# Retention with first ranks as tasks of a list scheduler, a state of 128 full partitions, and five warming products

## The chip, the cores and the metric

The kernel runs on one core of a Trainium2 chip. Its time is device time in microseconds (us), from a launch to its end. Five engines have their own instruction streams, each run strictly in order: TensorE (PE; its weight loads PEld), VectorE (DVE), ScalarE (ACT), GpSimd (POOL) and SyncE (SP). An engine that waits for a value holds up everything behind it in its stream. DMAs are issued from SyncE's queue above all.

## What is computed

Three layers, one behind the other. Retention over 2 batches, 8 heads, 768 positions, 64 columns per head; then a mixture of 8 experts over 1536 tokens of 512 columns, in which each expert gets exactly 192 tokens; then a dense layer with ELU.

```python
for b in range(nb):                       # retention, per batch and head
    intra = einsum('bhic,bhjc->bhij', qb, kb) * Dmask   # lam ** (i - j), i >= j
    intra = einsum('bhij,bhjd->bhid', intra, vb)
    inter = einsum('bhid,bhde->bhie', qb * lam_pow, kv_state)
    out[:, :, sl] = intra + inter
    kv_state = lam_block * kv_state + einsum('bhsd,bhse->bhde', kb * rev_pow, vb)

logits = x @ w_gate                       # experts
for idx in argsort(-logits.flatten()):    # greedy: best pairs first, 192 per expert
    ...
for e in range(E):
    out[mask] = maximum(x[mask] @ w1[e], 0) @ w2[e]

h = x @ w_in                              # dense
out = where(h > 0, h, exp(minimum(h, 0)) - 1) @ w_out
```

## The kernel before

**Tiling.** Retention goes over 12 chunks of 128 positions (6 per batch; n is the chunk, c its number within the batch). Per chunk k and q are transposed on TensorE and copied out by ScalarE (kT, qT); `scores` makes 8 products of 64 rows into two banks; VectorE masks them with the decay (`masks`); `inter` multiplies the running state with the scaled q (qS); `intra` adds the masked scores times v; `state` multiplies the decayed k (kD) with v, and VectorE adds the result to the decayed old state (`new_state`, sD). The state is kept as 128x128 blocks per pair of heads, of which only the two 64x64 corners are filled; so it is written in two steps of 64 partitions, and `inter` is 4 full products. ScalarE copies the output (xT), TensorE turns it back (`natural`, xN), and it goes to DRAM (xd).

**First ranks.** A token's rank is the count of tokens whose best logit beats its own. So per chunk `scored` makes 8 logits per token, `logits` copies them and finds the best logit m and its expert (four small VectorE steps: m, t, wv, oh), `new_row` spreads m over all partitions (mrow), `compare_new` and `compare_old` compare the new chunk with all earlier ones, and `count` sums the comparisons on TensorE.

**Dense pieces.** w_in and w_out are 64 bit; 16 pieces of 1 MB are loaded (`load_dense`) and split into a high and a low half (`split_steps`: three VectorE steps, one copy on ScalarE, one VectorE step). Three pieces are split beside the retention, two more are loaded there, and the rest is done among the experts.

**Order.** In the retention the order of VectorE and TensorE is written out by hand: each function gets an offset from its chunk's number, and the steps are sorted by it (`steps`). ScalarE, GpSimd and SyncE follow from the program's general order. Behind that, `Plan` sets the order: a list scheduler with a cost per task, that takes at each step the task with the longest tail among those that can start soonest. Its ranks of expert 0 (`choose`) end in the index products (L835), ahead of which 12 warming products of ones stand in TensorE's stream (L872), and 16 behind.

**Tables.** The powers of lambda are made by doubling on VectorE (rt, L194), sent to DRAM (rtd) and read back as the scale of q (qsc); the decay matrix (dec, L202) comes from 8 scans. The loads of the second chunk stand behind these on SyncE's queue.

## Time and profile before

| | |
|---|---|
| median of 3 runs (lowest, highest) | 545.36 us (544.83, 548.29) |
| the profiled execution, and its span | 544.31 us, 542.5 us |
| busy in the span: TensorE, its weight loads | 512.8 us (95%), 434.9 us (80%) |
| busy in the span: VectorE, ScalarE, GpSimd | 372.0 us (69%), 290.0 us (53%), 103.2 us (19%) |
| chain that ended last, by engine | TensorE 64%, VectorE 14%, DMA 7%, issue 5%, ScalarE 4%, GpSimd 3% |

The busy share is a mean over stages with different limits, so each stage is read by itself. The chain of work is followed back from the last instruction to what released it. A row of windows names the busy time of TensorE, its weight loads, VectorE, ScalarE and GpSimd in this order, then the granted clock as a share of 2.4 GHz. "Idle before" is time for which an engine stood still ahead of an instruction, with what ended it.

### The profile page before, as it was taken

The page shows a single profiled execution, that of the slowest core. Times are in us where ns is not written, and L with a number is a line of the kernel's source. Part 1 is how long each engine was busy: PE and PEld are TensorE (multiplying, and loading weights), DVE is VectorE, ACT ScalarE, POOL GpSimd, SP SyncE. Part 2 cuts the span into 40 slices and gives each one's busy share as a digit, 9 for nine tenths or more (in the row PEclk, how much of TensorE's full clock was granted, in tenths as well). Part 3 has the DMA queues.
Part 4 walks back from the last instruction along what each step waited for, and adds up shares of the span by engine and source line. Part 5 has one row for each costly group of instructions (what it writes and reads, how often), then busy time and mean ns, then how long its engine had stood idle before and what let it go on. Part 6 is the DMA issues. An engine that isn't in the chain of part 4 may idle for free.

```text
span 542.5 us, 12848 instructions
## 1 busy us (share of the span) xinstructions
PE 512.8 (95%) x5308; PEld 434.9 (80%) x5308; DVE 372.0 (69%) x847; ACT 290.0 (53%) x556; POOL 103.2 (19%) x143
## 2 busy tenths in 40 slices
PE   6989899889899989999999999999999999999994
PEld 5878888879899975569959964997898489879941
DVE  7499899797989979698477665747647653572410
ACT  2335442332894584363984595459539533961910
POOL 5232420200116500230343010012401001000000
PEclk9899989799899999999999999999999999999999
DMA  6998961287486610460541045051405505050000
GB/s 133 242 226 205 263 214 46 69 279 323 132 292 218 225 33 2 185 212 3 187 141 44 17 171 174 22 185 22 158 4 187 174 21 185 3 174 2 2 19 21
DMA packets 62763, 70.70 MB, mean 130 GB/s; under 512 B 40184, under 2 KB 45264, under 8 KB 61680
## 3 DMA queue, kind: packets, MB, share of 16 engines
q1 hardware_dynamic: 59744, 63.21, 36.8%
q0 software_dynamic: 2960, 6.66, 3.6%
q8 instruction: 42, 0.69, 0.5%
q14 instruction: 17, 0.14, 0.1%
HBM read 63.34 MB, written 6.52 MB: 129 GB/s over the span
## 4 chain that ended last, share of the span: by engine, by line
PE 64%; DVE 14%; DMA 7%; issue 5%; ACT 4%; POOL 3%; SPq 0%; POOLq 0%; ACTq 0%
PE ps_s L981 5%; PE ps_s L980 5%; PE ps_t L981 5%; PE ps_s L982 4%; PE ps_t L980 4%; PE ps_t L982 4%; PE ps_s L1150 3%; PE ps_s L1148 3%; PE ps_s L1149 3%; PE ps_t L1148 2%; PE ps_t L1149 2%; PE ps_t L1150 2%; PE ps_S L980 2%; PE ps_S L981 2%; PE ps_S L982 2%
## 5 line engine op out<-in xcount | busy, mean ns | idle before, releaser
L981 PE MATMUL ps_t<-yt,wih 128*128 128x192 f16 x208 | 51.4, 247 | 1.6 <-DVE yt L1067 1.6
L982 PEld LDWEIGHTS <-wil 128*128 128x128 f16 x512 | 50.4, 99 | 1.8 <-issue 1.7
L982 PE MATMUL ps_t<-yt,wil 128*128 128x192 f16 x208 | 51.5, 248 | 0.0
L980 PE MATMUL ps_t<-yt,wih 128*128 128x192 f16 x208 | 51.4, 247 | 0.0
L980 PEld LDWEIGHTS <-wih 128*128 128x128 f16 x512 | 50.7, 99 | 0.1
L981 PEld LDWEIGHTS <-wih 128*128 128x128 f16 x512 | 50.4, 99 | 0.2
L982 PE MATMUL ps_s<-yt,wil 128*128 128x192 f16 x200 | 49.7, 248 | 0.0
L981 PE MATMUL ps_s<-yt,wih 128*128 128x192 f16 x200 | 49.7, 248 | 0.0
L980 PE MATMUL ps_s<-yt,wih 128*128 128x192 f16 x200 | 49.7, 248 | 0.0
L668 POOL DMA_INDIRECT open<-rec,dest x27 | 34.4, 1274 | 57.8 <-DVE dest L657 26.4
L1150 PEld LDWEIGHTS <-gg 128*128 128x128 f16 x192 | 18.8, 98 | 23.5 <-DVE gg L1129 0.9
L1150 PE MATMUL ps_s<-woh,gg 128*128 128x512 f16 x96 | 36.4, 379 | 0.4 <-DVE gg L1129 0.4
L1149 PE MATMUL ps_s<-wol,gg 128*128 128x512 f16 x96 | 36.4, 379 | 0.0
L1148 PE MATMUL ps_s<-woh,gg 128*128 128x512 f16 x96 | 36.4, 379 | 0.0
L1129 DVE TENSOR_TENSOR gg<-el,gg 128x384 f16<-128x384 f32 x64 | 34.4, 553 | 1.7 <-ACT gg L1128 1.6
L1121 ACT ACTIVATE el<-el 128x384 f32<-128x384 f32 x64 | 33.5, 524 | 1.8
L1122 ACT ACTIVATE el<-el 128x384 f32<-128x384 f32 x64 | 33.5, 523 | 1.7
L972 DVE SCALAR_TENSOR_TENSOR w2p<-stg,w2p 128x1024 f16<-128x1024 f32 x24 | 28.4, 1224 | 8.6 <-ACT w2p L969 8.5
L1128 ACT ACTIVATE gg<-el 128x384 f16<-128x384 f32 x64 | 31.6, 511 | 5.1 <-DVE el L1123 4.8
L1149 PEld LDWEIGHTS <-gg 128*128 128x128 f16 x192 | 18.7, 98 | 19.0
L1148 PEld LDWEIGHTS <-gg 128*128 128x128 f16 x192 | 18.8, 98 | 18.9
L860 POOL DMA_INDIRECT xa<-xd,idx x8 | 8.6, 1078 | 129.1 <-DVE idx L841 128.5
(254 smaller groups left out, 1561.5 us busy)
## 6 DMA issues: line engine op xcount, KB each, us to landing
stg<-in_moe_w_dram SPq DMA_DIRECT2D x24, 1024.0 KB, 5.4
stg<-in_moe_w_out_dram SPq DMA_DIRECT2D x8, 1024.0 KB, 4.9
stg<-in_moe_w_in_dram SPq DMA_DIRECT2D x5, 1024.0 KB, 6.3
w1p<-in_moe_w_dram SPq DMA_DIRECT2D x8, 512.0 KB, 5.8
w2p<-in_moe_w_dram SPq DMA_DIRECT2D x8, 512.0 KB, 8.8
kn<-in_k_dram SPq DMA_DIRECT2D x12, 256.0 KB, 4.9
qn<-in_q_dram SPq DMA_DIRECT2D x12, 256.0 KB, 5.0
vn<-in_v_dram SPq DMA_DIRECT2D x12, 256.0 KB, 4.6
```

Source lines behind the costliest of these rows:

```text
L668: st = nc.gpsimd.indirect_dma_start(out=buf, out_offset=bass.IndirectOffsetOnAxis(ap=dest[:, c:c + 1], axis=0), in_=rec[:, c, :], in_offse ...
L972: nc.vector.scalar_tensor_tensor(part(1), T["t"][:, 1024 * z:1024 * z + 1024], sc, part(0), op0=OP.mult, op1=OP.subtract)
L980: nc.tensor.matmul(o, wh, xh, start=first, stop=False, skip_group_check=True)
L981: nc.tensor.matmul(o, wh, xl, start=False, stop=False, skip_group_check=True)
L982: nc.tensor.matmul(o, wl, xh, start=False, stop=last, skip_group_check=True)
L1121: a = add("ACT", 0.49, lambda: nc.scalar.activation(e_, e_, AF.Exp, scale=-1.0), a, ahead=EAHEAD)
L1122: a = add("ACT", 0.49, lambda: nc.scalar.activation(e_, e_, AF.Copy, scale=SG, bias=-SG), a, ahead=EAHEAD)
L1128: a = add("ACT", 0.49, lambda: nc.scalar.activation(gh, two(e_), AF.Copy), a, *free, ahead=EAHEAD)
L1129: a = add("DVE", 0.53, lambda: nc.vector.tensor_tensor(gl, two(e_), gh, op=OP.subtract), a, ahead=EAHEAD)
L1148: nc.tensor.matmul(p, GH[:, f, c], woh[:, f, :], start=f == 0, stop=False, skip_group_check=True)
L1149: nc.tensor.matmul(p, GH[:, f, c], wol[:, f, :], start=False, stop=False, skip_group_check=True)
L1150: nc.tensor.matmul(p, GL[:, f, c], woh[:, f, :], start=False, stop=f == RF2 - 1, skip_group_check=True)
```

## The change

**What it does.** Retention and first ranks become tasks of a second `Plan` (hp), for all five engines. `Plan.add` gets a mode: a task of another mode than the last one on its engine costs 0.12 more in the plan, and one of the same mode is preferred by 0.5. (1) The power table goes; the scale of q comes from 4 scans over lambda, loaded as lam2 by ScalarE's queue, as lambda and w_gate are too. (2) The state is kept as 128 partitions of 4 x 64 columns, so `new_state` and the decayed state are one step each, and `inter` is 8 products of 64 rows by 64 columns, into two banks; heads of odd pairs come out swapped, and `natural` turns them back with a permuted identity (swap). xT is copied in two halves. (3) The scaling of k goes from GpSimd to ScalarE, 8 activations of 128x64 a chunk; the scaling of q goes from VectorE to GpSimd. (4) Per chunk VectorE finds m alone; wv and oh come for groups of 4, 4, 3 and 1 chunks (`best`). (5) Five dense pieces are split beside the retention, two more loaded. (6) Ahead of the retention 10 warming products stand in place of 16; ahead of the index products of expert 0, 5 in place of 12. (7) Of the two copies of a whole expert's tokens (xt) the second goes to VectorE. (8) The zero fill on GpSimd takes 2 x 64 columns of a chunk's slots in place of all 320.

```diff
-EARLY = ((0, 1.35), (2.45, 3.8), (6.1, 7.25))
-NEXT = (8.3, 9.3)
-WARM = (12, 4, 12, 16)
+EARLY_N, NEXT = 5, 2
+LD, PITCH, BEHIND = (1.3, 1.1), 5.5, 2.0
+WARM = (10, 5, 16)
...
+    TURN, KEEP = 0.12, 0.5
...
-            t = max(near, key=lambda t: tail[t["n"]] + t["ahead"])
+            t = max(near, key=lambda t: tail[t["n"]] + t["ahead"] + (self.KEEP if mode.get(t["eng"]) == t["mode"] else 0.0))
...
+    lamb = consts.tile([128, H], FT)
+    nc.scalar.dma_start(lamb, bass.AP(tensor=lam.tensor, offset=lam.offset, ap=[[0, 128], [1, H]]))
+    lam2 = consts.tile([128, HP], FT)
+    for i in range(2):
+        nc.scalar.dma_start(lam2[64 * i:64 * i + 64], bass.AP(tensor=lam.tensor, offset=lam.offset + i, ap=[[0, 64], [2, HP]]))
...
-    while w < 128:
-        nc.vector.tensor_scalar(rt[:, O + w + 1:O + 2 * w + 1], rt[:, O + 1:O + w + 1], rt[:, O + w:O + w + 1], None,
-                                op0=OP.mult)
-        w *= 2
...
+    def q_scales():
+        for a in range(HP):
+            nc.vector.tensor_tensor_scan(qsc[:, a, :], lam2[:, a:a + 1].to_broadcast([128, 128]), nothing, 1.0,
+                                         op0=OP.mult, op1=OP.add)
...
+        for h in range(4 * z, 4 * z + 4):
+            nc.scalar.activation(KD[n][:, h, :], KN[n][:, h, :], AF.Copy, scale=dec[:, 4 * (h % 2) + h // 2, 127:128])
...
+        QS[n] = att.tile([128, HP, 128], FT, name="qS")
+        nc.gpsimd.tensor_tensor(QS[n], QT[n], qsc, op=OP.mult)
...
+        OP_[n] = p = bank("o"), bank("m")
+        for a in range(HP):
+            for s in range(2):
+                r, z = slice(64 * s, 64 * s + 64), s ^ (a & 1)
+                nc.tensor.matmul(p[a % 2][64 * z:64 * z + 64, 128 * (a // 2):128 * (a // 2) + 128], Sb[n % NC % 2][r, a, :],
+                                 QS[n][r, a, :], start=a < 2, stop=False, skip_group_check=True)
...
+        if n % NC:
+            nc.vector.tensor_add(sn, pv, SD[n])
...
+    def best(c0, c1):
+        sh = [128, c1 - c0, E]
+        l, t = R.L[:, c0:c1, :], t4[:, 0:c1 - c0, :]
+        nc.vector.tensor_tensor(t, l, m[:, c0:c1, None].to_broadcast(sh), op=OP.is_equal)
         nc.vector.tensor_tensor(t, t, e8b.to_broadcast(sh), op=OP.mult)
+        nc.vector.tensor_reduce(wv[:, c0:c1], t, axis=AX, op=OP.max)
+        nc.vector.tensor_tensor(oh[:, c0:c1, :], wv[:, c0:c1, None].to_broadcast(sh), e8b.to_broadcast(sh), op=OP.is_equal)
...
+            put((e, n), "PE", 0.46, lambda n=n, z=z: transposed(n, z), *of(("ld", nm, n), (e + "o", n - 1)), mode="A")
+            put((e + "o", n), "ACT", 0.58, lambda n=n, z=z: transposed_out(n, z), *of((e, n), ("scores", n - 2), ("qS", n - 2)))
...
+        ld = add("SP", 2.9, lambda i=i: load_dense(i), T["ld", "v", 1], use[i % 2])
...
-            for _ in range(WARM[2]):
-                w = add("PE", 0.22, lambda: warm(), w)
+            for _ in range(WARM[1]):
+                w = add("PE", 0.43, lambda: warm(), w)
...
+                    (nc.vector.tensor_copy if g else nc.scalar.copy)(
+                        xt.rearrange("p a r n -> p (a r n)").bitcast(FT).rearrange("p (r n) -> p r n", r=RD)[:, sl, :], pv)
```

**ScalarE, the start of its stream, before** (kT and qT are the copies of transposed k and q, xT that of a chunk's output, L its logits, xN the natural order):

```order
L292 ACT_TABLE_LOAD
L292 ACTIVATE kT<-ps_t_186 128x512
L305 ACTIVATE qT<-ps_t_196 128x512
L292 ACTIVATE kT<-ps_t_222 128x512
L305 ACTIVATE qT<-ps_t_232 128x512
L351 ACTIVATE xT<-ps_o 128x512
L428 ACTIVATE L<-ps_m 128x8
L292 ACTIVATE kT<-ps_t_292 128x512
L305 ACTIVATE qT<-ps_t_302 128x512
L383 ACTIVATE xN<-ps_x 128x512
```

and now (kD is the scaled k, lam_74 the tile lam2; an x is a repeat):

```order
L156 DMA lamb<-in_lam_dram 128x8
L159 DMA lam_74<-in_lam_dram 64x4x1 x2
L198 DMA wg<-in_moe_w_gate_dram 128x2x8
L198 DMA wg<-in_moe_w_gate_dram 64x2x8 x2
L294 ACT_TABLE_LOAD
L294 ACTIVATE kD<-kn,dec 128x64 x4
L288 ACTIVATE kT<-ps_t_164 128x512
L294 ACTIVATE kD<-kn,dec 128x64 x4
L288 ACTIVATE qT<-ps_t_178 128x512
L294 ACTIVATE kD<-kn,dec 128x64 x4
L288 ACTIVATE kT<-ps_t_191 128x512
```

The six loads of lambda and w_gate come first, and the first chunk's k is scaled, four heads at a time, ahead of the copies of kT and qT; the second chunk's likewise.

**VectorE, from the masks of the fifth chunk to its new state, before** (wol is where masked scores lie, f a dense piece's scratch, stg its load, w1p the comparisons, S the state):

```order
L326 TENSOR_TENSOR wol<-ps_s_541,dec 128x512
L326 TENSOR_TENSOR wol<-ps_s_542,dec 128x512
L252 TENSOR_SCALAR f_136<-stg_134 128x1024
L431 TENSOR_REDUCE m<-L 128x1
L433 SCALAR_TENSOR_TENSOR t_567<-L,m,e_90 128x8
L434 TENSOR_REDUCE wv<-t_567 128x1
L435 TENSOR_SCALAR oh<-e_90,wv 128x8
L312 TENSOR_TENSOR qS<-qT,qsc 128x512
L255 SCALAR_TENSOR_TENSOR f_136<-stg_134,f_136 128x1024
L452 TENSOR_SCALAR w1p<-mrow,m 128x384
L448 SCALAR_TENSOR_TENSOR w1p<-mrow,m,before 128x128
L485 TENSOR_TENSOR w1p<-mrow,m 128x3x128
```

and now:

```order
L311 TENSOR_TENSOR wol<-ps_s_543,dec 128x512
L311 TENSOR_TENSOR wol<-ps_s_544,dec 128x512
L404 TENSOR_REDUCE m<-L 128x1
L411 TENSOR_TENSOR t_140<-L,m 128x32
L412 TENSOR_TENSOR t_140<-t_140,e_85 128x32
L413 TENSOR_REDUCE wv<-t_140 128x4
L414 TENSOR_TENSOR oh<-wv,e_85 128x32
L425 TENSOR_SCALAR w1p<-mrow,m 128x384
L453 TENSOR_TENSOR w1p<-mrow,m 128x3x128
L421 SCALAR_TENSOR_TENSOR w1p<-mrow,m,before 128x128
L243 TENSOR_SCALAR f_119<-stg_117 128x1024
L356 TENSOR_TENSOR S_126<-ps_S,sD 128x256
```

The scaling of q is gone, t, wv and oh are replaced by four steps for four chunks (here the group's end), the dense step stands elsewhere, and the state is one step of 128 partitions.

**TensorE, between the counts and the index products of expert 0, before** (ohs are the slots, mt the chosen tokens):

```order
L460 LDWEIGHTS woh
L460 MATMUL ps_S<-oh,woh 128x8
L777 MATMUL ps_o<-th,onesf 128x16
L872 MATMUL ps_t_1429<-onesf 128x128 x12
L835 LDWEIGHTS ohs
L835 MATMUL ps_o<-mt,ohs 128x1
```

and now:

```order
L433 LDWEIGHTS woh
L433 MATMUL ps_t_1171<-oh,woh 128x8
L819 MATMUL ps_o<-th,onesf 128x16
L914 MATMUL ps_t_1475<-onesf 128x128 x5
L877 LDWEIGHTS ohs
L877 MATMUL ps_o<-mt,ohs 128x1
```

Only the number of products of ones has changed there.

## Rows read from the trace of the kernel before

**Rows 1.** Windows: busy us by engine (instructions), clock, DMA share, GB/s.
```profile
27.71:95.73 68.02, 62.79 (x843) 57.56 (x843) 63.80 (x142) 27.78 (x61) 19.28 (x26) 0.95 0.70 188
20.00:68.00 48.00, 43.26 (x535) 39.80 (x533) 40.77 (x92) 21.91 (x48) 17.01 (x24) 1.00 0.95 237
```

**Rows 2.** Chain that ended last: start, us, what.
```profile
2.38 3.35 DVE rt L194
...
9.77 4.24 DMA qn<-in_q_dram
...
27.71 1.29 DVE wol L326 x2
...
86.89 1.29 DVE wol L326 x2
...
95.73 0.27 DVE tp L762
...
98.33 5.10 PE ps_t L872 x24
103.43 0.59 PE ps_o L835 x24
...
111.36 0.88 ACT xt L910 x2
```

**Rows 3.** Timeline: start, us, engine, line, operation, count, idle before.
```profile
7.36 2.61 DVE L202 TENSOR_TENSOR_SCAN dec<-lamb,identf 128x128 f32<-128x128 f32 x8
...
14.15 0.94 PE L303 MATMUL ps_t<-identf,qn 128*128 128x128 f32 x4 [2.05 <-DMA qn<-in_q_dram]
...
18.86 0.39 PE L389 MATMUL ps_m<-wg,xT 128*128 128x8 f32 x2
...
39.04 1.06 PE L389 MATMUL ps_m<-wg,xT 128*128 128x8 f32 x8
...
41.30 1.06 PE L335 MATMUL ps_o<-qS,S 128*128 128x128 f32 x8
...
43.88 1.16 PE L321 MATMUL ps_s<-qT,kT 64*128 64x128 f32 x16
44.97 1.06 PE L389 MATMUL ps_m<-wg,xT 128*128 128x8 f32 x8
...
100.45 0.17 DVE L822 TENSOR_TENSOR mt<-me,tid 128x12 f16<-128x12 f32 x1
```

**Rows 4.** VectorE lines: count, busy, mean ns, idle before; 0 to 95.7 us.
```profile
L312 DVE TENSOR_TENSOR qS<-qT,qsc 128x512 f32<-128x512 f32 x10 | 6.9, 687 | 4.7 <-ACT qT L305 4.7
L374 DVE TENSOR_TENSOR S<-ps_S,sD 64x256 f32<-64x256 f32 x16 | 6.7, 419 | 0.3
...
L435 DVE TENSOR_SCALAR oh<-e,wv 128x8 f16<-128x8 f32 x12 | 3.0, 246 | 0.4
L433 DVE SCALAR_TENSOR_TENSOR t<-L,m,e 128x8 f32<-128x8 f32 x12 | 2.9, 242 | 0.4
...
L434 DVE TENSOR_REDUCE wv<-t 128x1 f32<-128x8 f32 x12 | 1.9, 162 | 0.4
```

**Rows 5.** Windows of the dense pieces' scratch tile alone: VectorE and ScalarE.
```profile
27.71:95.73 68.02, 12.81 (x11) 3.18 (x3) 0.95 0.70 188
```

**Rows 6.** Lines of ScalarE, 0 to 95.7 and 96 to 112 us.
```profile
L292 ACT ACTIVATE kT<-ps_t 128x512 f32<-128x512 f32 x12 | 7.2, 597 | 12.4 <-PE ps_t L290 12.4
...
L795 ACT ACTIVATE far<-slots,rk 128x192 f32<-128x192 f16 x6 | 2.3, 447 | 0.9 <-DVE rk L763 0.9
```

**Rows 7.** Waits: who waited for whom: us in total, times, longest.
```profile
DVE f L252 <- DMA stg<-in_moe_w_in_dram: 5.5, 2, 3.6
...
POOL kD L296 <- DMA kn<-in_k_dram: 2.9, 2, 2.5
...
PE ps_t L981 <- DVE yt L1067: 1.6, 1, 1.6
```

**Rows 8.** Windows, one microsecond among the warming products, as rows 1.
```profile
102.00:103.00 1.00, 1.00 (x6) 1.00 (x6) 0.00 (x0) 0.00 (x0) 0.00 (x0) 0.50 0.66 185
```

More of the change, by code (lines that the diff above doesn't have):

```diff
@@ new lines, in state, with new_state @@
+    def state(n):
+        for h in range(H):
+            nc.tensor.matmul(hb[64 * (h % 2):64 * (h % 2) + 64, 64 * (h // 2):64 * (h // 2) + 64],
+                             KD[n][:, h, :], VN[n][:, h, :], start=True, stop=True, skip_group_check=True)
+    def new_state(n):
+        pv = hb[:, 0:256].rearrange("p (a b) -> p a b", a=HP)
+        sn = Sb[(n % NC + 1) % 2]
+        if n % NC:
+            nc.vector.tensor_add(sn, pv, SD[n])
+        else:
+            nc.vector.tensor_copy(sn, pv)
@@ L492 @@
     nc.vector.memset(a16[:, 1, 0:1], 0.0)
-    steps = []
-    for n in range(NT):
-        for f, o in ((scored, 1.0), (logits, 1.05), (k_transposes, -0.9), (q_transposes, -0.85), (q_scaled, -0.8),
-                     (natural, 1.25), (inter, 0.3), (new_row, 1.35), (intra, 0.4), (compare_new, 1.45),
-                     (compare_old, 1.46), (state, 0.5), (new_state, 0.55), (scores, -0.4), (masks, -0.35)):
-            if f is natural and n >= LATE:
-                o = 40 + n
-            steps.append((n + o, f, n))
-        if n > 1:
-            steps.append((n - 3, load, n))
@@ L526 @@
[L526 to L538 removed]
+    hp = Plan()
@@ new lines, with of, put, fed @@
+    add = hp.add
+    T = {}
+    def of(*keys):
+        return [T[x] for x in keys if x in T]
+    def put(key, *a, **b):
+        T[key] = add(*a, **b)
+    def fed(n):
+        for z, nm in enumerate(("k", "q", "v")):
+            put(("ld", nm, n), "SP", LD[n > 1], lambda n=n, z=z: load(n, z),
+                *of(*((("kT", n - 3), ("kD1", n - 3)), (("qT", n - 3),), (("intra", n - 3), ("state", n - 3)))[z]))
+    fed(0)
+    put("qsc", "DVE", 1.4, q_scales, ahead=100.0)
+    T["qsc"]["deps"].append((T["ld", "k", 0], 3.0))
@@ new lines, with said @@
+    for n in range(LATE, NT):
+        put(("nat", n), "PE", 0.45, lambda n=n: natural(n), *of(("xT0", n), ("xT1", n), ("xNo", n - 1)), mode="A")
+        put(("xNo", n), "ACT", 0.58, lambda n=n: natural_out(n), *of(("nat", n), ("keep", n - 2)))
+        put(("keep", n), "SP", 0.75, lambda n=n: natural_kept(n), *of(("xNo", n)), lag=1.0)
+    def said(c, t):
+        return T["below", c] if t < c else T["tie", c] if t == c else T["old", t, 5 * (c // 5) if c < 10 else c]
+    pairs = sorted([(c, t) for c in range(NT) for t in range(NT)], key=lambda x: (max(x), x))
@@ new lines, with go @@
+    last, at = T["qTo", NT - 1], 0
+    while at < len(pairs):
+        n = max(pairs[at])
+        some = [x for x in pairs[at:at + 6] if max(x) == n or n < NT - 1 and max(x) < NT - 1]
+        def go(some=some, first=at == 0):
+            if first:
+                cnt[0] = bank("t1")
+            for i, (c, t) in enumerate(some):
+                count(c, t, first=first and i == 0)
+        last = add("PE", 0.027 * len(some), go, last, *[said(c, t) for c, t in some],
+                   *[T["best", next(g for g in groups if g[0] <= c < g[1])[0]] for c, t in some], mode="A")
+        at += len(some)
@@ L539 @@
+    done = hp.order()
+    engines = {getattr(mybir.EngineType, x) for x in ("PE", "DVE", "Activation", "Pool", "SP")}
+    with tc.manual_schedule(engines=engines):
+        keep_warm("m", WARM[0])
+        for t in done:
+            t["fn"]()
     att_ctx.close()
@@ L1177 @@
     R.task = None
-    for i in range(EARLY_N, EARLY_N + len(NEXT)):
+    for i in range(EARLY_N, EARLY_N + NEXT):
         dense(i)
-    S_use = work.uses[4]
+    S_use = work.uses[2]
     gb, ga = choose(0, start, S_use)
```

359 lines of the change are left out of this document (156 added, 203 removed).

## The prediction

> **What bounds the kernel now.** I read the busy time by stretches first, then the chain of work that ended last, then single lines. The program has two stretches. In the first (retention and first ranks) the chain runs almost only over VectorE: from the third chunk's masks at 27.71 us to the first ranking step at 95.73 us VectorE is busy 63.80 of 68.02 us, with TensorE right behind it at 62.79 [rows 1, 2]. In the second, the experts, TensorE is the one that is hardly ever without work; its longest wait for VectorE's copies of the expert's output is 1.6 us [rows 7]. So the first stretch pays for VectorE's time, the second for TensorE's. Between them lies a bridge in which one thing waits for the next: ranks, chosen expert, index products, gather, copies of the tokens. In it the reader should see the 12 warming products that begin at 98.33 and hold TensorE for 5.10 us, until 103.43, although the input of the index products behind them was written by 100.45 + 0.17 = 100.62 us [rows 2, 3].
>
> The start of the first stretch is worse than its rest. A chain of small multiplications builds the powers of lambda (one of them takes 3.35 us), q of the second chunk is waited for over 4.24 us [rows 2], and VectorE stands still twice for a dense piece, 5.5 us together [rows 7]. The third chunk's masks start only at 27.71; in the even part behind that a chunk takes TensorE 44.97 - 39.04 = 5.93 us [rows 3].
>
> **Part 1, the start.** The power table and its way through DRAM go; scans take their place, 4 for the scale of q beside the 8 for the decay. Eight took 2.61 us [rows 3], so twelve take 3.9. The first four wait for lambda, whose third load is ScalarE's third issue. Its landing has no row: between at once (1.6 us, two issues in) and q's 4.24 us after that [rows 2], so 1.6 to 5.8; I take 4.0, nearer to the row of a load. With 0.5 for the identity the decay is complete at 8.4 us, six of its eight columns at 7.8. Now ScalarE has four scalings of k *ahead* of the first copy of transposed k, and four more ahead of q. Such a scaling (128x64, factor from a tile) has no row either. The nearest is a 128x192 activation with an operand from a tile, 0.447 us; less 128 columns at 597/512 = 1.17 ns it is 0.30, and 0.447 x 64/192 = 0.15 is the bound below [rows 6]. I take 0.27, nearer to the row. So q is copied at 7.8 + 1.1 + 0.6 + 1.1 + 0.6 = 11.2 us. TensorE has mostly stood by then. In the old start it slowed after such a pause: after 2.05 us of waiting the stretch of transposes, intra, state and scores took 18.86 - 14.15 = 4.7 us [rows 3]. I take the first scores at twice their 1.09 (44.97 - 43.88), 2.2 us: first masks at 13.4, the second 4.7 later at 18.1, the third after one chunk at 5.93 less row and natural order (0.6): 23.4 us. Loads of k and q for two chunks are now asked for ahead of any v, so I expect none late here. Against 27.71 that is 4.3 us ahead, 2.5 to 6 with the bounds of lambda's landing.
>
> **Part 2, VectorE from the third masks to the first ranking step.** It was busy 63.80 us [rows 1]. What changes in it: (a) two more dense pieces and the first step of piece one, 9 steps at 12.81/11 = 1.16 us [rows 5]: +10.5. (b) Scaling q goes to GpSimd, 8 x 0.687 [rows 4]: -5.5. (c) The new state is one step of 128 partitions in place of two of 64, 8 x 0.419 [rows 4]: -3.4. (d) Of four small steps per chunk three (0.242, 0.162 and 0.246 us [rows 4]) become four steps per group of chunks, at 0.2 each between those rows: -11 x 0.65 + 16 x 0.2 = -4.0. Together 61.4 us. Of the 4.22 us idle, the second wait for a dense piece (5.5 - 3.6 = 1.9 [rows 7]) should go; 2.3 stay. And the work isn't even. From the last masks to the first ranking step it was 95.73 - 86.89 = 8.8 us [rows 2]; two dense steps now stand there as well, 11.1. The other 50.3 us spread over nine chunks, 5.6 each, a little under TensorE's 5.93, so that TensorE sets these: 9 x 0.34 = 3.1 us. First ranking step at 23.4 + 61.4 + 2.3 + 3.1 = 90.2 us: **gain 5.5**.
>
> What this costs elsewhere. GpSimd was busy 19.28 of 68.02 us [rows 1]; it loses the scalings of k and gets eight products there, covered even at three times VectorE's 0.687. Queued behind them is only the decayed state. ScalarE gets 8 x 0.27 = 2.2 us a chunk, on top of two copies at 0.6, two half copies at 0.4, one in natural order at 0.6, logits and row at 0.5 and its dense part at 0.4 on average: 5.7 of 5.93 us. It is covered, but narrowly, and logits, rows and the next k queue behind those scalings (rivals A and B). Inter goes from 4 full products (1.06 us) to 8 of a quarter's size. Its bounds are the scores, 8 products of half the rows in 1.16 us, and half of that [rows 3]; I keep 1.06. The two ends would move the chunk by +0.1 or -0.5 and the sum by +0.9 or, since VectorE's 5.6 comes next, -3.1.
>
> Half the rows cost more than half the time in that row. The Trainium skill, TensorEngine Tiling (Array Packing), Key Properties, says that tiles load and multiply independently, four of 64x64 side by side, and that each change of tiling mode drains TensorE. By its first half inter would take about a quarter of eight full products, some 0.5 us, and the chunk 5.4. By the second half this change adds two drains a chunk. No row here prices a drain.
>
> **Part 3, 5 products in place of 12.** They ran at the lower level, granted 0.50, that is 1.2 GHz [rows 8]: 12 took 5.10 us, so 5 take 2.1, and end before the index input is there. The index products start at about 100.8 by the old clock of events rather than at 103.43: 2.6. They then run at the lower level themselves (0.59 us at the higher): -0.3. **Gain 2.3.** What covers the lower clock: 16 more products stand behind the index products while the gather is under way, at 0.43 each if need be 6.8 us, and the higher level came within 5.1 us of steady products before. Without that cover the first expert would begin at 1.2 GHz and lose about what 12 products bought, 2.6.
>
> **Part 4, one of the two copies of the tokens goes to VectorE.** They took 0.88 us one after the other [rows 2], side by side 0.5. I take half of the 0.4, as a dense step can stand ahead of it on VectorE: **0.2**.
>
> **Part 5, the experts.** Two dense pieces, 8 x 1.16 = 9.3 us of VectorE, leave this stretch; TensorE's wait of 1.6 us [rows 7] hangs on ScalarE's copy as well. I take **0.5**, bounds 0 and 3.5 (that wait, and as much again for a clock that falls in it).
>
> **Sum.** 5.5 + 2.3 + 0.2 + 0.5 = 8.5 us. The profiled execution took 544.31 us (its span is 542.5), so 535.8; the median of the runs shown is 1.05 above it: 536.9, said as **537**. Its own range, 533 to 540, has a chance of 0.58.
>
> **Rivals.**
> A, another engine paces the chunks (0.18). For it: from 20 to 68 us the DMA engines are busy 0.95 of the time, at 237 GB/s [rows 1]. A chunk moves four times 256 KB and on average 5/12 of a 1 MB piece, 1.49 MB, in 5.93 us 251 GB/s. Held to 237 a chunk takes 6.3 us, 0.36 more over nine chunks: 3.3; two drains a chunk of 0.2 or scalings at 0.32 would do the same to TensorE or ScalarE. Against it: loads are asked for two to three chunks ahead. The first gain is then 2.2 and part 5 nothing: 544.31 - 4.7 + 1.05 = 541.
>
> B, slower (0.08): ScalarE's queue stops for k. GpSimd waited up to 2.5 us for a load of k [rows 7], with nothing behind it that was needed. The wait moves with the scaling to ScalarE, ahead of logits, rows and copies, at a quicker pace of loads. At 2.5 us each it has eaten the 8.5 us with the fourth time, and from the sixth the kernel is slower by over 1%: 544.31 - 8.5 + 15 + 1.05 = 552. Against it: such a wait came twice in ten chunks.
>
> C, better (0.16): inter overlaps (-1) and the waits among the experts go (-3): 533, down to 530.
>
> From C to A the range is 531.5 to 543. A measurement of this kernel can tell about 1% from no change, so faster is below 539.9: 0.58 x 0.95 + 0.16 = 0.71; within 1% 0.21; slower 0.08.
>
> **What would show it.** Right: third masks at 22 to 25.5 us; first ranking step at 88 to 93; a scaling of k at 0.24 to 0.35; VectorE under 2 us without a dense piece; five warming products in 2.2 us, index products 5 us behind the first ranking step (7.7 before). Wrong: ScalarE waiting for loads of k, or VectorE for logits in most chunks (A, B); a chunk of over 6.3 us; the first expert's products at 1.2 GHz; new waits of over 2 us among the experts.

## The result, and the profile after the change

| | before | changed kernel |
|---|---|---|
| median (lowest to highest) of the paired runs | 545.94 us (544.83 to 548.29) | 538.61 us (538.41 to 539.30) |
| ratio to before, 95% interval | | 0.9862 [0.9827, 0.9897] |
| profiled execution, its span | 544.31 us, 542.5 us | 538.41 us, 536.6 us |
| third masks | 27.71 us | 26.60 us |
| first ranking step | 95.73 us | 95.70 us |
| from it to the first expert's products | 17.05 us | 14.29 us |
| from there to the end of the span | 429.72 us | 426.61 us |

The forecast was 537.0 us in a range of 531.5 to 543.0 us. The time lies inside it, 1.6 us above the forecast. The places don't agree, though. Of the 8.5 us in the sum, 5.5 were to come from the retention, which gained nothing; the 5.9 us by which the span shrank come from the bridge (2.8, forecast 2.5) and the experts (3.1, forecast 0.5). So two questions are open: what ate the retention's gain, and why the experts gained so much.

The chain of the changed kernel, from the start to the third masks (start, us, what):

```profile
1.98 7.67 DMA lam<-in_lam_dram
...
10.12 1.03 DVE qsc L191 x3
11.15 0.12 DVE identf L165
...
11.53 0.34 DVE dec L184
...
11.90 1.29 ACT kD L294 x4
13.20 0.48 ACT kT L288
13.68 0.95 ACT kD L294 x4
14.63 0.49 ACT qT L288
...
15.17 2.08 PE ps_s L307 x16
...
26.62 0.67 DVE wol L311
```

The reader should see one small load, lam2 (the decay per head, laid out for the scale of q), that lands at 9.65 us, and a queue behind it: four scans for the scale of q, then the identity, then the decay, then on ScalarE the scaling of k ahead of the copy of transposed k. The decay has eight columns. The first was ready at 11.87 us, all eight at 14.08 us, where 8.4 was forecast for all eight:

```profile
11.45 2.63 DVE L184 TENSOR_TENSOR_SCAN dec<-lamb,identf 128x128 f32<-128x128 f32 x8
```

The stretch behind it, VectorE's lines by shape there (count | busy, mean ns of one | idle before), and a place in the timeline of GpSimd and of VectorE. The first row is the whole stretch: busy time of TensorE, its weight loads, VectorE, ScalarE and GpSimd, then clock, DMA share and GB/s.

```profile
26.60:95.70 69.10, 63.16 (x939) 54.28 (x939) 66.26 (x117) 44.04 (x130) 17.60 (x15) 0.96 0.79 221
```
```profile
L246 DVE SCALAR_TENSOR_TENSOR f<-stg,f 128x1024 uint32<-128x1024 uint32 x5 | 7.2, 1430 | 0.0
...
L421 DVE SCALAR_TENSOR_TENSOR w1p<-mrow,m,before 128x128 f16<-128x128 f32 x4 | 3.4, 854 | 0.0
...
L421 DVE SCALAR_TENSOR_TENSOR w2p<-mrow,m,before 128x128 f16<-128x128 f32 x5 | 2.7, 545 | 0.0
...
L453 DVE TENSOR_TENSOR w1p<-mrow,m 128x384 f16<-128x384 f32 x1 | 1.3, 1310 | 0.5 <-ACT mrow L444 0.5
```
```profile
29.25 1.90 POOL L298 TENSOR_TENSOR qS<-qT,qsc 128x512 f32<-128x512 f32 x1 [2.53 <-ACT qT L288]
```
```profile
28.80 1.22 DVE L246 SCALAR_TENSOR_TENSOR f<-stg,f 128x1024 uint32<-128x1024 uint32 x1
29.93 1.37 DVE L421 SCALAR_TENSOR_TENSOR w1p<-mrow,m,before 128x128 f16<-128x128 f32 x1
31.23 0.27 DVE L428 TENSOR_SCALAR w1p<-mrow,m 128x128 f16<-128x128 f32 x1
```

VectorE was busy 66.26 us where 61.4 was forecast. Its diagonal comparison (L421, 128x128) took 0.55 to 0.85 us on average in the first two groups; before the same step took 0.346:

```profile
L448 DVE SCALAR_TENSOR_TENSOR w2p<-mrow,m,before 128x128 f16<-128x128 f32 x5 | 1.7, 346 | 0.0
```

In the timeline GpSimd's multiplication for q begins at 29.25, in the middle of a dense step on VectorE, and takes 1.90 us where an undisturbed one takes 1.27 or 1.28. The comparison begins at 29.93, in the middle of that multiplication, and ends at 31.30, just behind it (31.15).

### The profile page after: what moved, and what is told of

It reads as the page before. It is cut to its first block, busy times and chain, and to the rows that moved or that the text cites. A ratio compares the mean times of both kernels' runs of the same rounds, so it can differ in the third digit from the quotient of the medians.

```text
span 536.6 us, 12988 instructions
## 1 busy us (share of the span) xinstructions
PE 508.5 (95%) x5362; PEld 426.4 (79%) x5362; DVE 360.3 (67%) x807; ACT 307.5 (57%) x646; POOL 93.2 (17%) x124
## 3 DMA queue, kind: packets, MB, share of 16 engines
q10 hardware_dynamic: 1248, 0.02, 0.1%
## 4 chain that ended last, share of the span: by engine, by line
PE 66%; DVE 15%; issue 6%; DMA 5%; ACT 5%; POOL 1%; POOLq 0%; ACTq 0%; DVEq 0%
PE ps_t L1022 5%; PE ps_s L1023 5%; PE ps_t L1023 5%; PE ps_s L1022 5%; PE ps_s L1024 5%; PE ps_t L1024 5%; PE ps_s L1192 3%; PE ps_s L1190 3%; PE ps_s L1191 3%; PE ps_S L1022 2%; PE ps_S L1023 2%; PE ps_S L1024 2%; PE ps_t L1190 2%; PE ps_t L1192 2%; PE ps_t L1191 2%
## 5 line engine op out<-in xcount | busy, mean ns | idle before, releaser
L710 POOL DMA_INDIRECT open<-rec,dest x27 | 32.6, 1206 | 51.1 <-DVE dest L699 18.3
```

Source lines behind the costliest of these rows:

```text
L710: st = nc.gpsimd.indirect_dma_start(out=buf, out_offset=bass.IndirectOffsetOnAxis(ap=dest[:, c:c + 1], axis=0), in_=rec[:, c, :], in_offse ...
```

## Experiments

All are the changed kernel with one edit, but for two that start from one of the others, and one from the kernel before. The times of the places come from one profiled execution each; the ratio is to runs of the kernel before on the same chip. Those runs had medians of 546.4 to 547.6 us, where the result above had 545.94, so between experiments the ratios compare better than the medians.

| kernel | third masks | ranking step | bridge | experts | median us | ratio [95%] |
|---|---|---|---|---|---|---|
| lam2 made on the core | 19.97 | 89.30 | 14.63 | 426.87 | 534.76 | 0.980 [0.977, 0.983] |
| lam2 loaded by rows | 23.99 | 93.10 | 14.50 | 426.80 | 536.24 | 0.981 [0.978, 0.984] |
| scans for q behind dec | 24.36 | 93.46 | 14.28 | 427.86 | 537.65 | 0.983 [0.979, 0.986] |
| q not scaled | 26.61 | 91.57 | 14.45 | 427.38 | 536.00 | 0.982 [0.978, 0.986] |
| q scaled twice | 27.30 | 102.49 | 14.70 | 428.51 | 548.31 | 1.003 [1.001, 1.005] |
| q scaled on VectorE | 27.00 | 95.44 | 14.31 | 428.65 | 540.27 | 0.985 [0.980, 0.989] |
| three dense pieces early | 26.80 | 95.86 | 14.56 | 433.28 | 547.39 | 1.000 [0.997, 1.004] |
| two pieces left out | 27.30 | 94.38 | 14.28 | 429.94 | 538.36 | 0.983 [0.981, 0.985] |
| lam2 on the core, four pieces | 20.38 | 91.68 | 14.48 | 427.14 | 535.26 | 0.979 [0.976, 0.982] |
| lam2 on the core, six pieces | 19.96 | 91.67 | 14.62 | 426.61 | 536.35 | 0.980 [0.978, 0.982] |
| twelve warming products | 25.16 | 94.25 | 14.58 | 427.27 | 539.14 | 0.988 [0.985, 0.991] |
| before, five warming products | 27.85 | 101.23 | 14.30 | 427.77 | 543.01 | 0.991 [0.988, 0.995] |

"Bridge" is from the ranking step to the first expert's products, "experts" from there to the end of the span.

**The start: lam2 made on the core.**

```diff
-    for i in range(2):
-        nc.scalar.dma_start(lam2[64 * i:64 * i + 64], ...)
     def q_scales():
+        for i in range(2):
+            nc.vector.tensor_copy(lam2[64 * i:64 * i + 64], lamb[64 * i:64 * i + 64, i:H:2])
```

> The changed kernel with lam2 (the decay of each head, arranged for 128 partitions of two heads) made on the core: VectorE copies it from lamb in two steps of 64 partitions by 4, and the two loads of single elements are gone. In the changed kernel the load of lam2 took 7.67 us from 1.98 us on and VectorE's scans for the scaling of q waited 8.2 us for it; the first masks came at 17.27 us and the third at 26.60 us (forecast 23.4). Theory 'the load of lam2 ate the gain at the start': the scans start about 5 us earlier (4 to 5 us instead of 9.7 us), the third masks come at 23 to 24.5 us, the first ranking step at 92 to 94 us instead of 95.70 us, and the time falls by 2 to 3.5 us to about 535.5 us. Rival 'the loads of k and q or TensorE's low clock hold the start anyway': the scans start earlier, the third masks stay within 1 us of 26.6 us, and the time stays at 538 us. A second rival, 'VectorE is not what paces the stretch behind': the third masks come earlier by 2 us or more, the first ranking step doesn't.

Measured: third masks at 19.97 us, 6.6 us earlier, ranking step 6.4 earlier, time 534.76 us. The theory holds, and the effect is more than the expected 2.1 to 3.6 us at the third masks. Three rows say why: the microsecond from 6 to 7 us (busy by engine, then clock, DMA share, GB/s), first of the changed kernel, then of this one, and the first scores of this one in its chain:

```profile
6.00:7.00 1.00, 0.00 (x0) 0.00 (x0) 0.00 (x0) 0.00 (x0) 0.00 (x0) 1.00 0.26 48
```
```profile
6.00:7.00 1.00, 0.96 (x8) 0.88 (x8) 1.00 (x5) 0.38 (x2) 0.00 (x0) 1.00 1.33 215
```
```profile
9.88 1.16 PE ps_s L307 x16
```

First, beside the single elements the DMA engines bring little of the next loads (48 against 215 GB/s). Second, in the changed kernel TensorE has nothing to do from 5.6 to 11.3 us, and from 9 us on its granted clock is 0.50, the level of 1.2 GHz, up to and behind the first scores:

```profile
14.00:16.00 2.00, 1.69 (x12) 1.28 (x13) 0.27 (x3) 2.00 (x9) 0.00 (x0) 0.50 1.36 245
```

So the first scores took 2.08 us; with lam2 made on the core the clock stays at 1.00 in this execution and they take 1.16. That part isn't sure either way. The kernel with four pieces below also makes lam2 on the core and gives TensorE the same work up to the scores, yet its clock falls to 0.50 from 10 us on; the one with twelve warming products loads lam2 as the changed kernel does, and its clock is back before the scores. Their first scores:

```profile
9.79 2.08 PE ps_s L307 x16
```
```profile
15.06 1.16 PE ps_s L307 x16
```

The third masks differ by it: 20.38 against 19.97 us, and 25.16 against 26.60. So of the 6.6 us up to 1.4 can be the clock of one execution; the rest is the load. The gain at the start is carried on whole: 6.4 us at the ranking step, 5.8 in the span of the profile. That profiled execution is the fastest of its six; the medians, which weren't measured side by side, differ by 3.9, the ratios by 0.6%, some 3.4 us.

**The form of the load.** The same two loads, but of whole rows.

```diff
-        nc.scalar.dma_start(lam2[64 * i:64 * i + 64], bass.AP(..., offset=lam.offset + i, ap=[[0, 64], [2, HP]]))
+        nc.scalar.dma_start(lam8[64 * i:64 * i + 64], bass.AP(..., offset=lam.offset, ap=[[0, 64], [1, H]]))
```

> The changed kernel with the same two loads for lam2 in the same place of the same queue, to the same 64 partitions each, but of a head's whole row of 8 numbers (32 bytes in a piece) instead of 4 single numbers two apart; VectorE then picks the four with two copies of 64 x 4 (0.16 us each, as in the kernel with lam2 made on the core). Theory 'the 512 single elements are slow': 128 pieces land as fast as lamb's 128 rows (3.3 us from issue), the scans start at about 5 us, the third masks come at 20 to 21.5 us and the time is 533.5 to 536.5 us, as without the loads. Rival 'a load that is issued second, next to the first chunk's k and q, is late whatever its form': the landing stays at 6 to 8 us from issue, the third masks at 25 to 27 us, and the time is 537.5 to 540 us.

```profile
1.91 3.87 DMA lam<-in_lam_dram
5.81 0.18 DVE lam L192
...
8.14 1.29 ACT kD L297 x4
...
11.40 2.08 PE ps_s L310 x16
```

The load now takes 3.87 us in place of 7.67, in the same place of the same queue: the single elements were 3.8 us of it. The third masks come at 23.99 us only, since the decay is still 1.5 us later than without the load, and TensorE's clock has fallen in this execution by then (scores 2.08 us). So the theory holds for the load and half for the start.

**The queue behind the load.** The loads stay; the scans for the scale of q go behind those of the decay.

```diff
     nothing = consts.tile([128, 128], FT)
-    nc.vector.memset(nothing, 0.0)
+    nc.vector.tensor_scalar(nothing, dec[:, 7, :], 0.0, None, op0=OP.mult)
```

> The changed kernel with its loads as they are and only VectorE's order at the start changed: the zeros that the scans for the scaling of q read are now made from the last scan of dec (one 128 x 128 step in place of a fill), so that identf and the eight scans of dec, which need lamb alone, stand ahead of the four scans that wait for lam2. Theory 'the late load costs by what is queued behind it on VectorE': lam2 still lands at about 9.65 us, but dec is ready at 7 to 7.5 us, ScalarE's first scaling of k starts at 5 to 6 us and not 11.90 us, TensorE's clock stays at 1.00, the first masks come at 10.5 to 12 us, the third at 19.5 to 21 us, the first ranking step at 88.5 to 91 us, and the time is that of the kernel with lam2 made on the core, 0.98 of the kernel before (534 to 536 us). Rival 'the load itself (single elements on the DMA queues beside the first chunk's k and q) holds the start': the first masks stay at 15 us or later, the third at 24 us or later, and the time at 537 us or above.

```profile
0.77 3.33 DMA lamb<-in_lam_dram
...
4.12 7.14 DMA kn<-in_k_dram
...
12.48 2.01 PE ps_s L307 x16
```

ScalarE scales k from 5.96 us on, as expected, but now the second chunk's k, issued at 4.12 us, lands only at 11.26 us. That isn't the late issue: with lam2 loaded by rows the same k was issued at 4.09 us and took 3.8 us. The third masks at 24.36 us and the time of 537.65 us lie where the rival put them, the first masks (14.52 us) a little ahead of its 15. So the load itself holds most of the start. The order on VectorE is worth 2.2 us of the 6.6; the rest is in what the single elements do to the loads next to them and in the clock (scores 2.01 us).

**GpSimd's scaling of q: left out, and doubled.**

```diff
     def q_scaled(n):
-        QS[n] = att.tile([128, HP, 128], FT, name="qS")
-        nc.gpsimd.tensor_tensor(QS[n], QT[n], qsc, op=OP.mult)
+        QS[n] = QT[n]
```

> The changed kernel without the scaling of q: the products with the state read q unscaled, so GpSimd's eight multiplications of 128 x 512 are left out (the values that come out are not those of the reference). VectorE's own program is not touched. In the changed kernel the diagonal comparisons of 128 x 128 with two inputs in SBUF took 0.55 to 1.37 us on VectorE where before they took 0.35 us, and its work between the third masks and the first ranking step was 66.3 us where 61.4 us was forecast. Theory 'GpSimd's multiplications slow VectorE's steps that read two operands from SBUF': the diagonal comparisons fall to 0.35 to 0.45 us, the sign steps of the dense pieces fall by 0.05 to 0.2 us each, VectorE's work in the stretch falls by 4 to 6 us, the first ranking step comes at 90 to 92.5 us, and the time is 533 to 536 us. Rival 'VectorE's steps are slower for another reason (DMA writes into SBUF, the new shapes)': they keep their durations within 0.05 us; the first ranking step moves by less than 1 us.

```diff
         nc.gpsimd.tensor_tensor(QS[n], QT[n], qsc, op=OP.mult)
+        spare = att.tile([128, HP, 128], FT, name="spare", bufs=1)
+        nc.gpsimd.tensor_tensor(spare, QT[n], qsc, op=OP.mult)
```

> The changed kernel with GpSimd's scaling of q done twice, the second time into a spare tile that nothing reads; order and work of the other engines are as they were. Theory 'GpSimd's multiplications slow VectorE's steps': VectorE does nothing more, yet its work between the third masks and the first ranking step rises by another 3 to 6 us from 66.3 us, and the time by 3 to 6 us, to 541.5 to 544.5 us. Rival 'another reason': VectorE's durations stay, and the time stays within 1 us of 538.4 us, since GpSimd, with 17.6 us of work in 69 us, has room for eight more steps of 1.3 us.

The stretch from the third masks to the ranking step without the multiplications, and VectorE's lines in it:

```profile
26.61:91.57 64.96, 61.80 (x939) 53.78 (x939) 60.15 (x118) 43.77 (x130) 5.81 (x7) 0.97 0.86 236
```
```profile
L246 DVE SCALAR_TENSOR_TENSOR f<-stg,f 128x1024 uint32<-128x1024 uint32 x5 | 6.1, 1217 | 0.0
...
L420 DVE SCALAR_TENSOR_TENSOR w2p<-mrow,m,before 128x128 f16<-128x128 f32 x5 | 1.7, 340 | 0.0
...
L420 DVE SCALAR_TENSOR_TENSOR w1p<-mrow,m,before 128x128 f16<-128x128 f32 x4 | 1.4, 346 | 0.0
...
L452 DVE TENSOR_TENSOR w1p<-mrow,m 128x384 f16<-128x384 f32 x1 | 0.6, 558 | 0.5 <-ACT mrow L443 0.5
```

And with them doubled:

```profile
27.30:102.49 75.19, 64.71 (x939) 55.50 (x939) 71.82 (x117) 44.27 (x130) 30.12 (x23) 0.95 0.74 202
```
```profile
L423 DVE SCALAR_TENSOR_TENSOR w1p<-mrow,m,before 128x128 f16<-128x128 f32 x4 | 4.4, 1108 | 0.0
...
L423 DVE SCALAR_TENSOR_TENSOR w2p<-mrow,m,before 128x128 f16<-128x128 f32 x5 | 3.7, 746 | 0.0
```

VectorE's program is the same in all three, and its busy time is 60.15, 66.26 and 71.82 us with none, eight and sixteen multiplications on GpSimd. Every step for which a row is shown comes back without them to about the length it had in the kernel before (0.340, 0.346, 1.217 and 0.558 us). So one multiplication that GpSimd takes costs VectorE 6.1/8 = 0.76 or 5.6/8 = 0.70 us; doing it itself would cost 0.69. The rival (another reason) falls. Left out, the ranking step comes 4.1 us earlier, not 6.1, since TensorE's 61.80 us of work are then close to the whole stretch (64.96). Doubled, the step comes 6.8 us later and the time rises by about 9.7 us, where 3 to 6 were expected. VectorE's own 5.6 us lie in that range. Of the 9.1 us by which the span rose, 0.7 come from the start, 6.1 from the stretch, 0.4 from the bridge and 1.9 from the experts, which begin at the lower clock in this execution (0.51 and 0.63 from 116 to 120 us). Whether the doubling does that isn't shown.

**The scaling of q back on VectorE.**

```diff
-        nc.gpsimd.tensor_tensor(QS[n], QT[n], qsc, op=OP.mult)
+        nc.vector.tensor_tensor(QS[n], QT[n], qsc, op=OP.mult)
-            put(("qS", n), "POOL", 1.3, lambda n=n: q_scaled(n), ...)
+            put(("qS", n), "DVE", 0.69, lambda n=n: q_scaled(n), ...)
```

> The changed kernel with the scaling of q back on VectorE (128 x 512 by the scale, 0.69 us each), still as a task of the scheduler; GpSimd keeps the small scaling of the state. Without GpSimd's multiplications VectorE worked 60.2 us between the third masks and the first ranking step, with them 66.3 us. Theory 'putting them on GpSimd frees on VectorE what it costs there': VectorE's work comes to 60.2 + 8 x 0.69 = 65.7 us, its comparisons of 128 x 128 take 0.35 us again, the first ranking step moves by less than 1.5 us from 95.7 us and the time is 537 to 540 us. Rival 'the multiplications on GpSimd are a gain all the same, since they run in VectorE's waits': the step moves to 97 us or later, and the time is 540 to 542 us. Rival 'the contention costs more than the steps themselves': 94 us or earlier, and 535 to 537 us.

```profile
27.00:95.44 68.44, 61.40 (x939) 53.40 (x939) 64.17 (x126) 44.31 (x130) 5.14 (x7) 0.95 0.78 218
```

The ranking step comes at 95.44 us, 0.3 earlier than in the changed kernel: the first theory. VectorE's 64.17 us are 1.5 less than it expected, and 2.1 less than with the multiplications on GpSimd. The median is 540.27 us, just above its 537 to 540; the interval of the ratio overlaps that of the changed kernel, and so the times can't be told apart. Moving this work to GpSimd cost VectorE at least what it took away.

**The dense pieces: three early, and two left out.**

```diff
-EARLY_N, NEXT = 5, 2
+EARLY_N, NEXT = 3, 2
```

> The changed kernel with three dense pieces beside the retention in place of five (as before the change); the other two go to the experts' part. A piece is four steps on VectorE, 5.2 to 5.4 us in the changed kernel. Theory 'VectorE paces the retention, and the two pieces moved there cost what they take': VectorE's work between the third masks and the first ranking step falls by about 10 us to 56 us, the step comes 5 to 9 us earlier (TensorE has 63 us of work in the 69 us), and the products of the experts take 2 to 4 us more than the 426.6 us of the changed kernel, as they did before (429.7 us): 532 to 537 us. Rival 'TensorE paces it at once': the step comes less than 3 us earlier, the experts lose 3 us, and the time stays at 538 us. Rival 'the two pieces are what the experts' part gained by': the step earlier by 5 us, the experts longer by 5 us or more, and the time at 538 us or above.

```diff
             def go(z, i=i, P=P):
+                if i in (3, 4):
+                    return
```

> The changed kernel with the steps of two of the five dense pieces (the fourth and the fifth) left out: their places in the order of all engines stay as they are, their loads still run, and their parts of wih and wil are zeros written at the start (so the experts compute with zeros there and the values are not those of the reference). This takes 8 steps of VectorE, about 10.5 us, and 2 of ScalarE out of the retention, without the other order that the scheduler found for three pieces, where VectorE had 58.1 us of work, not 66.3 us, and the first ranking step still came at 95.86 us. Theory 'VectorE's work paces the retention, and with three pieces only the order was worse': the step comes 4 us or more earlier, at 88 to 91.7 us (TensorE's 63 us of work set the end then), and the time is 531 to 535 us. Rival 'the chain from chunk to chunk through TensorE and ScalarE paces it, and VectorE's freed time becomes waits': the step comes less than 2 us earlier than 95.7 us, and the time stays at 536.5 to 538.5 us.

Three pieces: VectorE's work in the stretch falls from 66.26 to 58.06 us, and the step doesn't come earlier (95.86 us). The third theory is nearest for the experts, which take 6.7 us more; only the second theory (less than 3 us) had left room for a retention that gains nothing. The order of the scheduler is another one here, so the second run takes the two pieces out without touching it. Its step comes at 94.38 us, 1.3 earlier, and 2.0 if the later start (0.7, from a longer low clock) is taken off; the time is 538.36 us. As worded that is the rival, with less than 2 us and 536.5 to 538.5. Its experts hold two drops of the clock, 1.7 us each, so the time isn't a clean measure. From 70 to 90 us, first of the changed kernel, then of the one without two pieces:

```profile
70.00:90.00 20.00, 19.52 (x304) 16.68 (x302) 19.79 (x33) 10.25 (x27) 5.06 (x4) 1.00 0.48 162
```
```profile
70.00:90.00 20.00, 20.00 (x324) 17.57 (x325) 14.12 (x30) 9.15 (x28) 3.74 (x4) 1.00 0.63 199
```

The left-out steps stood behind 69 us. VectorE has 5.7 us less to do there, but TensorE now has work at every moment. So two bounds lie closely one above the other: VectorE until the multiplications or pieces go, and TensorE some 2 to 4 us below it (2.0 here, 4.1 without the multiplications).

**Four and six pieces,** with lam2 made on the core, by the same number.

> The kernel with lam2 made on the core, with four dense pieces beside the retention in place of five. With three in place of five (and lam2 loaded) the first ranking step did not move and the experts took 6.7 us more; with lam2 made on the core and five pieces the step came at 89.30 us and the time was 534.8 us. Theory 'pieces beside the retention lie in waits that are there anyway, and one that moves to the experts costs some 3 us there': the step comes at 88 to 90 us, the experts take 2 to 4 us more than 426.9 us, and the time is 536.5 to 539 us. Rival 'VectorE paces the retention at five pieces and no longer at four': the step comes 3 us or more earlier, and the time stays at 533 to 536 us.

> The kernel with lam2 made on the core, with six dense pieces beside the retention in place of five (four more steps of VectorE, 5.4 us, in 69.3 us where it works 66.5 us). Theory 'VectorE is full at five': the first ranking step comes 2.5 to 5 us later than 89.30 us, the experts take 0 to 3 us less than 426.9 us, and the time is 535 to 539 us. Rival 'a sixth piece still finds waits to lie in': the step moves by less than 1.5 us, the experts gain 1.5 to 3 us as they did from three to five pieces, and the time is 531.5 to 534 us.

Four and six pieces both move the ranking step to 91.7 us from 89.3, and the experts stay within 0.3 us of 426.87. For four pieces the step was expected to stay or come earlier, so both theories miss; VectorE's work fell to 60.37 us and the stretch took 71.30, in an order that the scheduler made anew. For six the time fits the first theory, and the step, 2.4 us later, is just short of its 2.5. With four pieces the start (0.4) and the experts (1.7) hold a low clock that five and six don't show. The times, 535.26 and 536.35 us, can't be told from five pieces (ratios 0.979, 0.980 and 0.980). Five is no sharp optimum; only three, with lam2 loaded, is too few.

**Warming products.** Twelve again in the changed kernel, and five in the kernel before.

```diff
-WARM = (10, 5, 16)
+WARM = (10, 12, 16)
```

> The changed kernel with twelve warming products again in place of five. The forecast put 2.3 us on the seven that went; the two traces show the index products 2.7 us nearer to the ranking step. Theory 'the seven products stood in the path and nothing else hangs on them': the index products come 2.3 to 2.8 us later, the experts take as long as in the changed kernel, and the time is 540.7 to 541.2 us. Rival 'the shorter bridge is paid back elsewhere, or the gain in the experts hangs on it too (the drop of the granted clock at 140 to 150 us that only the kernel before shows)': the products of the experts then take some 1.5 to 2 us longer as well, and the time is 542 to 543.5 us; or, if TensorE enters the first expert at a lower clock with five products, the time rises by less than 1.5 us.

```diff
-WARM = (12, 4, 12, 16)
+WARM = (12, 4, 5, 16)
```

> The kernel before with one number changed: five warming products ahead of the first index products in place of twelve. Before, the index products began 2.82 us after VectorE had their input (100.45 to 103.27 us), behind the twelve products of 0.43 us at half clock; seven fewer are 3.0 us, of which 2.8 us can be had. Theory 'the gain of the bridge is these seven products and stands by itself': the index products begin 0.2 to 0.4 us after their input, the first expert's products about 2.5 us earlier, and the time is 542.5 to 544 us (from 545.9 us), with the drop of the granted clock at 140 to 150 us still there. Rival 'the drop in the experts comes from the bridge': the drop is gone as well, and the time is 541 to 542.5 us. Rival 'TensorE then waits for its clock later': its clock rises later than before, and the time stays above 544.5 us.

The products (L914 and L872, two records each) and the index products behind them: the changed kernel, the one with twelve, the kernel before with five.

```profile
98.08 2.48 PE L914 MATMUL ps_t<-onesf 128*128 128x128 f32 x10
100.37 0.81 PE L877 MATMUL ps_o<-mt,ohs 128*128 128x1 f16 x24
```
```profile
96.92 3.28 PE L914 MATMUL ps_t<-onesf 128*128 128x128 f32 x14
100.03 0.74 PE L877 MATMUL ps_o<-mt,ohs 128*128 128x1 f16 x24
```
```profile
103.67 2.48 PE L872 MATMUL ps_t<-onesf 128*128 128x128 f32 x10
105.94 0.82 PE L835 MATMUL ps_o<-mt,ohs 128*128 128x1 f16 x24
```

In the kernel before, five in place of twelve bring the index products to 0.27 us behind the start of the step that writes their input (2.82 before) and the bridge to 14.30 us (17.05): the 2.8 us by themselves, as the first theory says. The drop of the clock at 144 us, which that theory kept, is gone, as the rival has it. The median, 543.01 us, fits the first theory; the ratio, 0.991, is a gain of 3.0 to 6.8 us, so more than the bridge can be in it. The profiled execution has a ranking step 5.5 us later: VectorE waited 7.8 us for dense pieces, not 5.5, and TensorE's clock was low from 70 to 84 us (69 to 72 before). Its places in the retention can't be compared. In the changed kernel twelve did not cost the expected 2.3 to 2.8 us but 0.5 in the median and 0.2% in the ratio, whose interval overlaps. Here the scheduler put seven products ahead of the index products and five behind; these began 1.06 us behind that step, not 0.23, and the clock was back at 1.00 by 100 us, not 104.4. The bridge is only 0.3 us longer, so most of the 0.8 came back, by the clock as far as the rows show. So both theories had the wrong price: what costs is not their number alone but how many stand *ahead* of the index products.

## Why the prediction was right in the sum and wrong in its places

- **Part 1, the start (4.3, measured 1.1).** The failed step is lam2's landing: 9.65 us, where 4.0 was taken between 1.6 and 5.8. The upper bound was the duration of a load of 256 KB; 512 elements of 4 bytes took 7.67 us. What followed was told rightly in its order (decay, four scalings of k ahead of the copy, first masks). It came less late than lam2: the landing is 5.65 us behind the forecast, the first masks (17.27 us) 3.9, since the first scaling of k starts behind one column of the decay (11.90 us) and not behind six of eight. The scaling of k was right: 4 in 0.95 us, 0.24 each (forecast 0.27). First scores were 2.08 us (forecast 2.2); with lam2 made on the core two executions of three kept the clock, and in those the first masks come at 11.06 and 11.07 us (forecast 13.4). The early end of this part's range follows from its own sum as 4.3 + 2.4 = 6.7, not 6.
- **Part 2, the stretch to the ranking step (1.2 of the 5.5, measured -1.1).** The list of edits was right: without GpSimd's multiplications VectorE is busy 60.15 us (forecast 61.4). The failed step is (b), "scaling q goes to GpSimd: -5.5", and "covered even at three times VectorE's 0.687": GpSimd had the time, but its work isn't free for VectorE. It cost 6.1 us there, more than the 5.5 it took off: a term that the sum put at nothing. The second idle, for dense pieces, did go (no such wait is left). The 2.3 idle and 3.1 of TensorE's pace, 5.4, came out as 2.8.
- **Inter.** Of the two ends the better one was true: its 8 quarter products run in pairs side by side, in 23.73 - 23.07 = 0.66 us with start and end (forecast 1.06). No gain from it shows, with VectorE as the bound.

```profile
23.07 0.33 PE L320 MATMUL ps_o<-qS,S 64*64 64x128 f32 x2
23.08 0.33 PE L320 MATMUL ps_m<-qS,S 64*64 64x128 f32 x2
...
23.45 0.28 PE L320 MATMUL ps_o<-qS,S 64*64 64x128 f32 x2
```

- **Parts 3 and 4, the bridge (2.5, measured 2.8).** Right, and shown apart by the kernel before with five products (2.8). The copy of the tokens on VectorE gained nothing that can be seen: a dense step stands ahead of it, and from the last transposes to the first expert's products it is 109.99 - 108.27 = 1.72 us, before 112.78 - 111.11 = 1.67.
- **Part 5, the experts (0.5, measured 3.1).** The range of 0 to 3.5 held it, the value was too small. TensorE's wait for the copies of the first expert's output fell from 1.6 us [rows 7] to 0.8 (below). The other part is the clock: before, it fell at 144 us and cost 2 x 0.49 + 2 x 0.36 = 1.7 us; in the changed kernel it didn't. That makes 2.5 of the 3.1 us; the cause of the other 0.6 is open.

```profile
PE ps_t L1023 <- DVE yt L1109: 0.8, 1, 0.8
```
```profile
144.00:146.00 2.00, 2.00 (x16) 1.90 (x14) 1.93 (x3) 0.73 (x3) 1.31 (x2) 0.51 0.42 119
146.00:148.00 2.00, 2.00 (x18) 1.93 (x17) 1.97 (x3) 1.62 (x4) 0.00 (x0) 0.64 0.27 78
```

  Whether this drop belongs to the kernel before isn't settled. With five warming products the same kernel waited as long at that place (1.58 us) without a drop. So 1.7 of the 3.1 us may be chance. That fewer pieces among the experts are worth something is shown by the run with three early: 6.7 us more, of which one drop of the clock (0.66 over 5 us) is 1.7.
- **Rivals.** A (another engine paces the chunks) came nearest for the retention (a gain of 2.2 us, where none came), but its causes didn't hold: the DMA engines gave 261 GB/s from 20 to 68 us (237 before [rows 1]), ScalarE was busy 36.69 of 48 us. B fell: ScalarE waited for a load of k at the start only. C came true in its second half (waits among the experts) and in inter's overlap.

```profile
20.00:68.00 48.00, 45.47 (x640) 39.40 (x636) 42.13 (x74) 36.69 (x115) 14.53 (x14) 1.00 1.03 261
```

So the total was near by luck: two misses of 3.2 and 2.3 us in the retention met one of 2.6 us, the other way, in the experts. What the change could have given shows in the kernel with lam2 made on the core: 534.76 us, ratio 0.980 [0.977, 0.983]. That is clearly faster than the kernel before; against the changed kernel (0.986 [0.983, 0.990]) the two intervals just touch.

## What to carry to other kernels

Before work goes to an idle engine, ask what it shares with the one that is relieved: here 8 multiplications on GpSimd took at least as much of VectorE's time as VectorE would have needed for them. A small load isn't a cheap one: count its pieces, and see what stands in order behind whoever waits for it. TensorE's clock may or may not survive such a wait, so compare single executions with that in mind. Check a sum by place, since a right total can hide misses that cancel.

## What the runs showed of the hardware

In the rows above GpSimd and VectorE exclude each other rather than share. The comparison at 29.93 us ended 0.15 us behind GpSimd's multiplication, and that had itself waited for the dense step ahead (1.90 for 1.27 us). The masks, with one operand from PSUM, kept their length: 681 ns here, 686 in the stretch of the kernel before, and 1.28 us for the two from 51.27 us on, beside a multiplication that starts at 51.91. Two comparisons with one tensor operand from SBUF were held too (L428, 128x128): the pair took 1.88 us from 66.37 on and ended just behind GpSimd's multiplication (68.17); without the multiplications it took 0.84. So a second operand from SBUF isn't the only case. The Trainium skill, SBUF — State Buffer, section "Who interferes with whom" and the summary of rules, says that the two have one pair of ports in common, that a VectorE step with two SBUF inputs and a GpSimd step that reads SBUF lock it for a whole instruction, and that the later one fully blocks. The rows agree, and give the price here: 0.7 to 0.76 us of VectorE for each multiplication of 128x512.

The load of lam2 in single elements took 7.67 us, in rows of 32 bytes 3.87. In the first 14 us ScalarE's queue moved 1248 packets with the single elements, 864 with rows: 384 more, which is 512 elements less 128 rows. The Trainium skill, DMA: Bandwidth & Descriptors, "Rules for kernel authors", says that a last dimension with a stride becomes one descriptor per element; that agrees with the packets and with the longer load. That loads of k and q beside it slow down as well (7.14 us for the second chunk's k, 3.8 beside the rows) is seen in the rows only.

TensorE's granted clock falls now and then among the experts, behind waits between 0.6 and 3.1 us, to 0.66 over 5 us, 1.7 us a time. Of 14 profiled executions of 14 kernels five show it, one of them twice (a sixth begins the experts with such a drop), and others had the same waits without it. A difference of 2 us between two single profiles of this kernel can be that alone.
